# A new hand-written order of all instructions in a fused attention and MLP kernel

## The chip, the cores and the metric

The kernel runs on one core of a Trainium2 chip. The metric is the device time of one execution in microseconds (us); lower is better. A core has five engines that run their own instruction streams in order: TensorE (PE, with its weight loads PEld), VectorE (DVE), ScalarE (ACT), GpSimd (POOL) and SyncE (SP). Here SP only issues DMAs; ACT and POOL issue a few as well. A difference of 0.2%, 1.45 us here, is about what a measurement of this kernel can tell from none.

## What is computed

Block-sparse attention over 4 batches, 8 heads, 768 positions of 64 dimensions, and then an MLP on its output (3072 tokens of 512 features). A block of 32 queries sees its own and the neighbouring blocks, the first and the last block, and three sampled blocks whose numbers are an input; the first and the last block see everything.

```python
scores = scale * np.matmul(q, k.transpose(0, 1, 3, 2))
scores = np.where(mask, scores, -1000000000.0)
attn = np.exp(scores - max);  attn = attn / (sum + 1e-09)
x = (attn @ v).reshape(B * S, H * D)
h = x @ w_in
g = h * np.clip(h + 3.0, 0.0, 6.0) / 6.0
return g @ w_out
```

## The kernel before

All addresses, tiles and operations are fixed in small classes (lines 330 to 727); the order in which they are emitted is one long string, SCORE (line 45), and that string is all that sets the order on every engine and every DMA queue. A phrase names a piece of work and its steps:

```python
for phrase in SCORE.split(";"):
    who, *ops = phrase.split()
    for op in ops:
        works[who[0]][int(who[1:])].do(op)
```

Each engine call is wrapped so that it keeps this order on its engine (Ordered, line 308). An engine thus runs its own steps in the order of the string, and waits where the data or the buffer of the next step is not there yet, with everything behind it on that engine waiting too. How the steps of different engines stand to each other in the string matters only where they share data or a buffer.

The pieces are these.
- **k, Index (line 337).** samp and table load the sampled block numbers; index (line 355) is nine small VectorE instructions that turn them into block numbers for the gathers.
- **c0 to c21, Cache (line 377).** The keys and values of one group of queries, in a ring of two buffers (RING = 2), so cache n waits for the jobs of cache n - 2. kw, vw, kg, vg are plain loads. kc and kf copy keys from the cache before (kc_1 on VectorE). kr and vr gather the three sampled blocks: they first read three block numbers into registers of the issuing engine, from the raw numbers (kr_101, kr_011) or from index's result, and then issue three DMAs. vr reads the registers itself only if kr of the same block has not done so before it (line 431: `regs = self.regs.get(t) or registers(...)`).
- **q, Group (line 437).** A load of the queries and their scaling.
- **j0 to j43, Job (line 459).** Attention of 64 queries: s (32 small matmuls into two PSUM banks), mx (maxima, VectorE), e (exponentials, ACT), then either t and ca or cv (transposes through TensorE and a copy, j0 to j15) or tr and mv (transposes on VectorE and four DMAs, from j16 on), av (64 small matmuls), dn, ml, x, xh, xl (division and the split into a high and a low part). **d0 to d7, Dense (line 561)** do the same for the blocks that see everything, in two halves (s_0, s_1).
- **w0 to w31, Weight (line 660).** A weight arrives as float64 in one of three stage buffers (load, 512 KB), size (ACT) and bits_0, bits_1, bits_2 (VectorE) turn it into float32.
- **m0 to m95, Step (line 682).** 6 units of 512 tokens times 16 slices of the hidden layer: wh and wl split a weight tile into high and low (ACT; GpSimd, in some cases VectorE), h_0 and h_1 are 12 matmuls into the one PSUM bank `hid`, ga, gb, gh, gl make the activation and its two parts (ACT, VectorE, ACT, GpSimd), o_0 to o_3 are three matmuls each into the four OUT banks, which collect 16 steps. oc, os copy a finished bank out (os in two halves on ACT and VectorE), od, oe store it.

Which engine does a step stands in its digits: xl_1 and wl_x1 are VectorE's, xl_0 and wl_x0 GpSimd's; load_1 and k.._1.. are issued by ACT, 0 by SP, vw_2. and kw_2. by POOL. m0 needs the outputs of j0 to j7, so TensorE's dense matmuls can start only when eight jobs are through.

Of the kernel before, what the change touches and what calls it, by code (L numbers as in the profile page):

```python
# [56 lines left out]
    e_00; j4 t_1; j5 e_01; m1 wh_1; j3 av_1; q3 qs_0; j4 ca_0; j3 dn; c3 vw_20 vw_01; j6 s; j3 ml; w4 load_0; j5 e_10;  # L57
    c3 vr_01; c4 kw_20; w0 size; j5 t_0; j6 mx_0; c3 vw_22; j6 mx_1 e_00; c3 vr_00; j6 e_01; m1 wl_10; j3 x; j4 cv_1;
    j6 t_0; j3 xh; j5 ca_0; j4 av_0; j3 xl_1; c4 kr_000; w0 bits_0; j5 e_11; j4 av_1; w2 bits_2; j6 e_10; j5 t_1; j6
    e_11 cv_0; j2 xh; j6 t_1; j4 dn; j2 xl_1; c4 kw_01; j6 ca_1; w0 bits_1; q4 load_0; j5 ca_1; j7 s; w0 bits_2; c4  # L60
    kr_010; w4 size; j4 ml; m0 wh_0; w4 bits_0; j5 av_0; j7 mx_0; j5 av_1; j7 mx_1 e_00; c4 vw_01; j7 e_01; j5 dn; j4
    x; j7 e_10; c4 vw_02; j7 t_0; m1 wh_0; w5 load_0; j5 ml; w4 bits_1; j6 av_0; j4 xh; j7 ca_0; w4 bits_2; j6 av_1;
    j7 e_11; c4 vr_00; j4 xl_1; j7 t_1; j6 dn; j5 x; j6 ml; j5 xh; c4 vw_00; j7 ca_1; j6 x; j5 xl_0; j7 av_0; m0
    wl_01; q4 qs_0; j7 av_1; j6 xh; j7 dn ml; j8 s; c4 vr_01; j7 x; j6 xl_1; j7 xh; j8 mx_0; j7 xl_0; w6 load_0; j8
    mx_1 e_00; m1 wl_00; q5 load_0; m0 h_0; j8 e_01; w8 load_0; c5 kw_01; j8 e_10; c5 kw_20; j8 e_11 t_0; w5 size; j8
    t_1; m0 h_1; j8 ca_0; w5 bits_0 bits_1; j8 ca_1; j9 s; m0 ga gb; j8 av_0 av_1; j9 mx_0; m0 gh; m1 h_0; w5 bits_2;
    m0 gl; w6 size; j8 dn; w7 load_0; j9 mx_1; m1 h_1; c5 kr_010; j9 e_00 e_01; w6 bits_0; m2 wh_0; m0 o_0; m1 ga; m2
    wl_01; m0 o_1; j9 e_10; w6 bits_1; c5 kr_000; w8 size; m0 o_2; m1 gb; q5 qs_0; j9 t_0; w8 bits_0; m0 o_3; j9 e_11;
    w8 bits_1; m1 gh; j9 t_1; w6 bits_2; m2 h_0; m1 gl; j8 ml; m3 wh_0; w9 load_0; j8 x; w7 size; m3 wl_01; m2 h_1; j9
    ca_0; w7 bits_0; j9 ca_1; w8 bits_2; m1 o_0; m2 ga; w7 bits_1; j9 av_0; w10 load_0; m2 wh_1; j9 av_1; m2 gb; j10  # L70
    s; j9 dn; m2 gh; w7 bits_2; m4 wh_0; m1 o_1; m2 gl; j10 mx_0; w11 load_0; w9 size; c6 vw_00; m3 h_0; j10 mx_1; c5
    vw_00; j10 e_00; m4 wl_01; j10 e_01; c5 vw_02; m1 o_2; j10 e_10; c5 vr_00; w9 bits_0; j10 e_11; j9 ml; j10 t_0; w9
    bits_1; w10 size; m1 o_3; w9 bits_2; j10 ca_0; m3 h_1; m2 wl_11; w12 load_0; c5 vw_01; w10 bits_0; j10 t_1; c5
    vr_01; w10 bits_1; m3 ga; m2 o_0; w10 bits_2; m2 o_1; m3 gb; m5 wh_0; c6 kw_00; m2 o_2; j9 x; w11 size; w14
    load_0; m4 h_0; q6 load_0; j10 ca_1; w11 bits_0; c6 kr_000; w11 bits_1; m3 gh; m4 h_1; m3 gl; w12 size bits_0; m2
    o_3; m4 ga; m5 wl_01; j11 s; m3 wh_1; m4 gb wh_1; j10 av_0; m3 wl_11; m4 gh; j10 av_1; w11 bits_2; m5 h_0; j9 xh;
    m4 gl; j10 dn; j8 xh; w13 load_0; j11 mx_0; c6 kr_010; m5 h_1; j11 mx_1 e_00; j9 xl_0; w14 size; m4 wl_10; j11
    e_01; m3 o_0; w14 bits_0; q6 qs_0; c6 kw_01; m3 o_1; j11 e_10; j8 xl_1; m3 o_2; j11 e_11; w14 bits_1; m5 ga; j11
    t_0; w12 bits_1; m3 o_3; j11 ca_0; w12 bits_2; m4 o_0; w14 bits_2; m6 wh_0; w16 load_0; m4 o_1; m5 gb; w13 size;
    w15 load_0; m4 o_2; c6 vw_01; m6 wl_01; m5 wh_1; j11 t_1; m7 wh_0; w13 bits_0; m4 o_3; w13 bits_1; m5 gh; m6 h_0;  # L80
    w13 bits_2; j11 ca_1; m5 gl; j10 ml; w17 load_0; j10 x; j12 s; c6 vr_00; w16 size; m7 wl_01; m5 wl_10; m6 h_1; j12
    mx_0; w16 bits_0; j12 e_00; j11 av_0; w15 size; w16 bits_1; j11 av_1; m6 ga; w16 bits_2; m5 o_0; j12 e_01; m6 gb;
    w18 load_0; m5 o_1; c6 vw_02; j11 dn; m6 gh; c6 vr_01; j11 ml; m5 o_2; w17 size; j11 x; m6 gl; j12 t_0 mx_1; m5
    o_3; w17 bits_0; j12 e_10; q7 load_0; m7 h_0; w15 bits_0; m6 wh_1; w15 bits_1; j12 e_11; w15 bits_2; m8 wh_0; m7
    h_1; m6 wl_11; m7 wh_1; w19 load_0; w17 bits_1; m6 o_0; m7 ga; w17 bits_2; j12 t_1 ca_0; m6 o_1; m7 gb; w20
    load_0; j12 ca_1; c7 kw_00; m7 wl_11; j12 av_0; m7 gh; c7 kr_000; j12 av_1; m8 wl_01; j11 xh; m7 gl; j13 s; j10
    xh; q7 qs_0; m8 h_0; w18 size; j13 mx_0; c7 kw_01; w18 bits_0; j13 e_00; w18 bits_1; m6 o_2; j13 e_01; w19 size;
    j12 dn; m8 h_1; w18 bits_2; w19 bits_0; m9 wh_0; w21 load_0; m6 o_3; j10 xl_1; c7 kr_010; m8 ga; j12 ml; m9 wl_00;
    m7 o_0; j13 mx_1; m7 o_1; m8 gb; j13 e_10 e_11; w19 bits_1; j13 t_0; m8 wh_1; c7 vw_00; m9 h_0; j11 xl_1; c7
    vw_02; m8 gh; w19 bits_2; w20 size; m8 gl; j12 x; j13 t_1; w22 load_0; m9 h_1; j13 ca_0; c7 vr_00; w20 bits_0  # L90
# [731 lines left out]
```

## Time and profile before

| | us |
|---|---|
| median of three runs | 726.73 |
| the runs | 725.34, 726.73, 726.80 |
| the profiled execution | 728.81 |
| its span, first to last instruction | 727.0 |
| TensorE busy in it | 685.3 |
| VectorE, ScalarE, GpSimd busy | 378.7, 372.7, 370.9 |
| moved by DMA | 123.54 MB, mean 170 GB/s |

The span is what the profile shows; the profiled execution's own time has 1.8 us more around it, and it is 2.1 us above the median of the runs. TensorE is the busy engine, but matmuls are pipelined and overlap in the records, so its share says only where it stands still, not how fast it is. The page cuts the span into slices; below, stretches are chosen by hand, and time is counted from the first instruction.

### The profile page before, as it was taken

Reading aid. Unit: us, or ns where it says so; the run is one execution under the profiler, and the core shown is the slowest. Engines: PE = TensorE matmul, PEld = TensorE weight load, DVE = VectorE, ACT = ScalarE, POOL = GpSimd, SP = SyncE. Lnnn points to the kernel's source line nnn. Section 1 sums busy time; section 2 is a strip of 40 time slices with the busy share of each in tenths; the row PEclk is TensorE's granted clock in tenths of the full one; section 3 lists DMA queues with packets and bytes.
Section 4 is the critical chain, followed back from the end, with each engine's and each line's share of the span. In section 5 each row is a group of like instructions: output and inputs, shape, how many; then the busy total and the mean of one; then the engine's idle time right before and its main releaser. Section 6 shows DMA issues by size and latency. Waiting matters only on the chain.

```text
span 727.0 us, 19157 instructions
## 1 busy us (share of the span) xinstructions
PE 685.3 (94%) x7552; PEld 524.3 (72%) x7552; DVE 378.7 (52%) x782; ACT 372.7 (51%) x735; POOL 370.9 (51%) x301
## 2 busy tenths in 40 slices
...
GB/s 258 252 247 254 249 280 263 260 255 215 216 259 122 199 196 162 155 191 207 166 217 124 183 229 139 176 140 154 181 209 219 162 81 60 1 58 1 2 0 59
DMA packets 83118, 123.54 MB, mean 170 GB/s; under 512 B 10707, under 2 KB 61524, under 8 KB 83028
## 3 DMA queue, kind: packets, MB, share of 16 engines
...
q10 hardware_dynamic: 2048, 2.76, 1.1%
...
## 4 chain that ended last, share of the span: by engine, by line
PE 80%; DVE 6%; DMA 5%; SPq 4%; ACT 3%; issue 2%; ACTq 0%; DVEq 0%
PE hid L316 34%; PE out L316 33%; PE bank L316 8%; PE small L316 6%; SPq L316 4%; ACT p L316 1%; DMA stage<-w_out 1%; DVE m L316 1%; DVE w_in L316 1%; DMA pT<-p 1%; DMA stage<-w_in 1%; DMA kp<-kG 1%; DMA vp<-vG 1%; DVE rec L316 1%; DVE g L316 1%
## 5 line engine op out<-in xcount | busy, mean ns | idle before, releaser
L316 PE MATMUL hid<-x,whi 128*128 128x512 f32 x768 | 241.0, 395 | 2.1 <-ACT x L316 0.9
L316 POOL TENSOR_TENSOR glo<-g,ghi 128x512 fp32r<-128x512 f32 x96 | 128.2, 1336 | 150.9 <-ACT ghi L316 147.3
L316 POOL TENSOR_TENSOR wlo<-w_out,whi 128x512 fp32r<-128x512 f32 x90 | 117.7, 1308 | 112.1 <-ACT whi L316 96.4
L316 DVE SCALAR_TENSOR_TENSOR g<-g,hid 128x512 f32<-128x512 f32 x96 | 65.7, 685 | 207.4 <-ACT g L316 207.3
L316 PEld LDWEIGHTS hid<-x,whi 128*128 128x128 f32 x768 | 141.9, 188 | 38.8 <-issue 2.8
L316 PE MATMUL out<-whi,ghi 128*128 128x512 f32 x384 | 155.1, 404 | 0.0
L316 PE MATMUL out<-whi,glo 128*128 128x512 f32 x384 | 149.8, 390 | 0.0
L316 PE MATMUL hid<-x,wlo 128*128 128x512 f32 x384 | 149.7, 390 | 0.0
L316 PE MATMUL out<-wlo,ghi 128*128 128x512 f32 x384 | 149.7, 390 | 0.0
L316 ACT ACTIVATE g<-hid,half_b 128x512 f32<-128x512 f32 x96 | 66.0, 688 | 154.2 <-PE hid L316 130.5
L316 POOL TENSOR_TENSOR wlo<-w_in,whi 128x512 fp32r<-128x512 f32 x88 | 114.6, 1305 | 54.7 <-ACT whi L316 35.8
L316 ACT ACTIVATE p<-bank,m 128x256 f32<-128x256 f32 (+1 forms) x196 | 88.6, 492 | 60.1 <-DVE m L316 51.1
L316 DVE TENSOR_REDUCE m<-bank 128x2 f32<-128x512 f32 (+1 forms) x114 | 70.9, 643 | 47.9 <-PE bank L316 47.6
L316 PEld LDWEIGHTS out<-whi,ghi 128*128 128x128 f32 x384 | 72.0, 188 | 25.3 <-issue 10.1
L316 PEld LDWEIGHTS out<-whi,glo 128*128 128x128 f32 x384 | 72.1, 188 | 15.6
L316 PEld LDWEIGHTS hid<-x,wlo 128*128 128x128 f32 x384 | 72.1, 188 | 15.5
L316 PEld LDWEIGHTS out<-wlo,ghi 128*128 128x128 f32 x384 | 72.2, 188 | 13.2
L316 ACT CAST ghi<-g 128x512 fp32r<-128x512 f32 x96 | 59.6, 621 | 35.2 <-DVE g L316 24.0
L316 ACT CAST whi<-w_out 128x512 fp32r<-128x512 f32 x96 | 59.4, 620 | 30.7 <-PE out L316 26.9
L316 ACT CAST whi<-w_in 128x512 fp32r<-128x512 f32 x96 | 59.4, 619 | 28.1 <-PE hid L316 23.1
L316 DVE STREAM_TRANSPOSE p<-p 128x512 f32<-128x512 f32 (+1 forms) x88 | 54.8, 646 | 24.1 <-ACT p L316 20.9
L316 PEld LDWEIGHTS small<-vp,pT 128*32 128x32 f32 x2816 | 43.6, 110 | 24.8 <-issue 17.5
...
## 6 DMA issues: line engine op xcount, KB each, us to landing
vp<-vG SPq DMA_DIRECT2D x174, 130.0 KB, 3.3
...
kp<-kG SPq DMA_DIRECT2D x39, 256.0 KB, 3.5
stage<-w_in SPq DMA_DIRECT2D x16, 512.0 KB, 4.1
stage<-w_out SPq DMA_DIRECT2D x15, 512.0 KB, 4.4
...
```

Of the source, the lines that this page charges most:

```text
L316: return lambda *a, **k: tc.keep_in_program_order(op(*a, **k))
```

## The change

Only the string SCORE is replaced. The 2822 steps in it are the same 2822 with the same digits, so every operation keeps its engine, its tile and its queue; their order is new throughout. Of the diff the opening, the stretch around d3 to j24, and the end are shown; lines with a minus come first.

```diff
@@ -43,232 +43,201 @@
 SCORE = """
-    q0 load_1; c1 vw_21; k0 samp_0; q1 load_1; k0 table_0; c0 kw_10; k0 ident_0; w3 load_1; c0 kw_11 vw_11 kr_101
-    kr_011; k0 index; q1 qs_0; c1 kw_11; c0 vw_00 vw_02; w3 size; c0 kg_0; q0 qs_0; c1 kr_010 kc_1; w1 load_0; c1
-    vw_00; c0 vr_00; c1 kr_000; j1 s; j0 s; c0 vr_01; j0 mx_0; j1 mx_0; j0 e_00; w1 size; j0 mx_1; c0 vg_0; j0 e_01;
-    w1 bits_0; w2 load_0; c1 kf_0; w3 bits_0; j0 t_0; j1 mx_1; j0 e_10; c2 kw_01; j1 e_00; j0 cv_0; c2 kr_000; j0
-    e_11; w3 bits_1; j1 e_01; j0 t_1; j1 e_10 t_0 e_11; j2 s; j0 ca_1; c2 kr_010; j3 s; j0 av_0; j3 mx_0; c1 vw_02; j1
-    t_1; c2 kc_1; q2 load_0; j2 mx_0; c3 kw_01; j0 av_1; c1 vg_0; j2 e_00; c3 kr_010; w2 size; j2 e_01; w2 bits_0; j3
-    e_00; j2 mx_1; j1 cv_0; j2 e_10; c1 vr_00; j2 e_11; j3 mx_1; j2 t_0; j3 e_01; w1 bits_1; j2 ca_0; j0 dn; c1 vr_01;
-    q2 qs_0; j0 ml; w3 bits_2; j1 av_0; j3 e_10; j0 x; j3 t_0; c3 kr_000; j1 cv_1; j4 s; w1 bits_2; w2 bits_1; m0
-    wh_1; j1 av_1; j4 mx_0; j0 xh; m0 wl_10; j3 e_11; j2 t_1; j3 cv_0; c2 vw_02; w0 load_0; j1 dn; j2 ca_1; q3 load_0;
-    j1 ml; c2 vr_01; j3 t_1; j1 x; c3 kc_1; j1 xh; j2 av_0; j4 mx_1; j3 ca_1; j2 av_1; j4 e_00; j1 xl_1; c2 vw_01; j0
-    xl_1; j5 s; j4 e_01; c2 vr_00; j2 dn; j4 e_10; j2 ml; j4 e_11; j2 x; j4 t_0; j5 mx_0; c2 vw_00; j3 av_0; j5 mx_1
...
-    d3 loadk_1; m30 wh_1; d2 dn; m30 gh gl; m31 h_1; d2 ml; m30 wl_10; m29 o_0; d2 x; m31 ga; d3 s_0 loadv_1; d1 xl_0;
-    c11 kw_00 vg_0; d3 mx_00 mx_10 e_00 e_10 s_1 tr_00 tr_10; m29 o_1; d3 loadv_0 mx_01 mv_0; m29 o_2; d3 mx_11 e_01;
-    m29 o_3; m31 gb; d3 e_11 fd; m30 o_0; m31 gh; d3 tr_01 fe; m30 o_1; m31 gl; d2 xh; d3 tr_11; m33 wh_0; j22 s; d3
-    mv_1; m31 wh_1; m30 o_2; m31 wl_10; j22 mx_0; m30 o_3; j22 mx_1; m32 wl_00; m31 o_0; q13 load_0; j22 e_00; m31 o_1
-    oc_0; j22 e_01; d3 av_00; j22 e_10; m31 od_0; d3 av_10; j22 e_11; c12 vg_0; j23 s; j22 tr_0 tr_1; j23 mx_0; d3
-    av_01; j22 mv; d3 av_11; j23 mx_1 e_00; m31 o_2; j23 e_01; d3 dn; j23 e_10; q13 qs_0; c11 vw_01; j23 e_11; d3 ml
-    x; j24 s; m31 o_3; d2 xl_1; d3 xh; m32 wh_1; d3 xl_1; j24 mx_0; m32 h_0 wl_10; j24 mx_1; j23 tr_0; m32 h_1; m33
-    wl_00; j24 e_00; j23 tr_1; j24 e_01 e_10; j22 av_0; j23 mv; j24 e_11; j22 av_1; m32 ga; j25 s; m33 wh_1; m32 gb;
...
-    gb; m93 o_1; m94 wl_10 gh; m95 h_0; m94 gl; m95 h_1; m93 o_2; m95 ga; m93 o_3; m95 gb; m94 o_0; m95 wh_1 gh; m94
-    o_1; m95 wl_11; m94 o_2; m95 gl; m94 o_3; m95 o_0 o_1 oc_0 o_2 oc_1 od_0 o_3 os_2 oe_2 od_1 os_3 oe_3
+    w3 load_1 size; k0 table_0; w3 bits_0; c0 kw_10 kw_11; w3 bits_1; c1 kc_1; k0 ident_0 samp_0; c1 vw_21; c0 kr_101;
+    q1 load_1; c0 vw_02; k0 index; c0 vw_00; c1 vr_00 vr_01; c0 kg_0 vg_0 kr_011; q0 load_1 qs_0; j1 s; j0 s; j1 mx_0;
+    j0 mx_0; q1 qs_0; j0 e_00 mx_1 e_10; c1 kw_11; j1 mx_1; j0 e_11; j1 e_00; j0 e_01; j1 e_11; j0 t_0; c1 kr_010; w1
+    load_0; c1 vw_00; c0 vr_00; c1 vg_0 kr_000; c2 kw_01; c0 vr_01; j1 e_01; c1 kf_0; c0 vw_11; j0 t_1 cv_0; j1 t_0; j2
+    s mx_0 mx_1; j1 cv_0; j2 e_00; j1 e_10; w1 size; j3 s; w1 bits_0; c2 kc_1; j0 ca_1; j2 e_11; w0 load_0; c1 vw_02; c2
+    kr_000; c3 kr_000; q2 load_0; j3 mx_0; c3 kc_1; w3 bits_2; j1 t_1; j0 av_0 av_1; j1 cv_1; w1 bits_1; j0 dn; w1
+    bits_2; j3 mx_1; c2 kr_010; q3 load_0; j3 e_00; j2 e_10 e_01 t_0 ca_0; j3 e_01 t_0; j2 t_1; w0 size bits_0; j0 ml x
+    xh; j1 av_0 av_1 dn; j3 e_11; j1 ml; q2 qs_0; j2 ca_1; w2 load_0; c3 kr_010; j4 s; c2 vw_00 vr_00; c3 kw_01; j2 av_0
+    av_1; c2 vw_01; j3 cv_0; w2 size; j4 mx_0 mx_1; j0 xl_1; j2 dn; j3 e_10; j5 s; j4 e_00; m0 wh_1; j4 e_01 e_11; j1 x
+    xh; j4 e_10; j3 t_1 ca_1; j4 t_0; w4 load_0; c2 vw_02; w2 bits_0; j2 ml; w2 bits_1 bits_2; j2 x xh; q3 qs_0; j3
+    av_0; j4 t_1; j3 av_1; w0 bits_1 bits_2; j3 dn; j4 ca_0; j1 xl_1; j6 s mx_0 mx_1 e_00 e_10 e_11 e_01; c2 vr_01; j6
+    t_0; c3 vw_01 vr_00; j3 ml; j5 mx_0; c3 vr_01; j3 x; j5 e_00; j3 xh; j2 xl_1; j5 mx_1; q4 load_0; c3 vw_22; j4 cv_1;
+    c4 kr_010; j6 t_1; c4 kw_20; j6 cv_0; j5 e_01 t_0; j4 av_0 av_1; j5 e_10; m0 wh_0 wl_01; j6 ca_1; j4 dn ml; j3 xl_1;
+    c4 kr_000; j7 s; j4 x; j7 mx_0; w4 size; j5 e_11 t_1; m1 wh_1; j5 ca_0; j4 xh; j5 ca_1 av_0 av_1; j7 mx_1; j5 dn; j7
...
+    av_10 mv_1 av_01 av_11 dn; c11 vw_00; d3 loadk_1; c11 vw_01; d2 ml; d3 loadk_0; c12 kr_010; m28 o_2; d2 x; m31 h_0
+    h_1; d3 s_0 mx_00; c12 vw_00; d3 mx_10; m30 gh; m29 wl_10; m30 gl; m29 o_3 o_2; m30 wh_1; m31 ga; m30 wl_10; d3
+    loadv_0; m31 gb; d3 e_00 e_10 tr_00 tr_10; d1 xh; m29 o_0; d1 xl_0; d3 s_1; m30 o_3; d3 mx_01 mx_11 fd e_01 e_11
+    tr_01 tr_11; m29 o_1; c12 kr_000; m30 o_1; q12 qs_1; m31 wh_1; d3 mv_0; m31 wl_10; j22 s; d3 loadv_1 mv_1; m30 o_0
+    o_2; m31 gh gl o_0; j22 mx_0 mx_1; d2 xh; j22 e_00; m31 o_1; j22 e_01 e_11 e_10; d3 fe; j22 tr_0 tr_1; j23 s; q13
+    load_0; j23 mx_0 mx_1; c13 kr_010; d3 av_00 av_01 av_11; m32 wh_0; d3 av_10 dn ml x; j23 e_00 e_01 e_10; d2 xl_1;
+    j23 e_11; q13 qs_0; m31 o_3 o_2; d3 xh xl_1; m32 wh_1 wl_00; j22 mv; m33 wh_0; j24 s mx_0; m32 h_0 h_1; j24 e_00
...
+    wl_10 o_3; m94 ga; m95 wh_0 wl_00; m94 gb; m92 o_2 o_0; m93 o_1 o_2; m95 h_0 h_1; m94 gh wh_1 gl wl_10; m93 o_0; m95
+    ga wh_1 gb; m94 o_3 o_0 o_2 o_1; m79 od_0; m95 wl_11 gh gl o_3 o_0 os_3 oe_3 o_2 os_2 oc_0 od_0 o_1 oc_1 od_1 oe_2
 """
```

In the new opening the load of w3 and its size stand first on ACT, ahead of c0's two key windows (kw_10, kw_11). On VectorE w3's bits_0 and bits_1 and the copy c1 kc_1 stand ahead of index. On SP c1's gathers vr_00 and vr_01 stand ahead of c0's kg, vg and kr_011, and ahead of c1's own kr. From m0 h_0 on, TensorE's stream comes back from a step of attention to h or o 67 times in the new order and 79 times in the old one. Between d3 s_0 and d3 s_1 TensorE has no step before and three o after; between j23 s and j24 s it has d3 av_01, d3 av_11 and one o before, four d3 av and two o after. On VectorE m54 gb stood directly behind d4 dn, d4 ml, j30 xl_1 and d4 x; now it stands directly behind m53 gb, with d4 ml and d4 x after it. At the end, the last output bank is o_1 with oc_1 (one copy, one store of 256 KB) in place of o_3 with os_3 (two half copies, two stores).

## Rows read from the trace of the kernel before

**Rows 1.** Three stretches: length; busy PE, PEld, DVE, ACT, POOL; clock; DMA share; GB/s.

```profile
0.00:67.50 67.50, 37.85 (x864) 23.68 (x864) 36.00 (x89) 29.95 (x66) 6.15 (x12) 0.92 0.79 251
67.50:80.00 12.50, 12.19 (x144) 9.34 (x144) 7.28 (x15) 8.44 (x18) 4.25 (x4) 1.00 0.90 300
80.00:722.00 642.00, 635.04 (x6546) 491.28 (x6544) 334.62 (x678) 333.90 (x652) 360.48 (x285) 1.00 0.54 159
```

**Rows 2.** Waits of PE from 80 us on: us in total, times, longest.

```profile
PE small L316 <- DMA pT<-p: 2.2, 5, 0.7
PE bank L316 <- DMA kp<-kG: 1.5, 1, 1.5
PE bank L316 <- ACT p L316: 1.3, 1, 1.3
PE bank L316 <- DVE rec L316: 0.9, 1, 0.9
PE hid L316 <- DVE g L316: 0.9, 2, 0.6
```

**Rows 3.** The chain that ended last, whole span: start, us, engine, what, matmuls.

```profile
189.18 2.72 PE hid L316 x12
...
210.12 2.95 PE hid L316 x12
```

**Rows 4.** Timelines of DVE, then POOL, at 161 to 182 us: start, us, what.

```profile
163.19 1.79 DVE L316 SCALAR_TENSOR_TENSOR w_in<-stage,w_in 128x512 int32<-128x512 int32 x1
...
179.59 1.41 DVE L316 SCALAR_TENSOR_TENSOR w_out<-stage,w_out 128x512 int32<-128x512 int32 x2
...
163.14 1.30 POOL L316 TENSOR_TENSOR glo<-g,ghi 128x512 fp32r<-128x512 f32 x1
...
169.43 1.74 POOL L316 TENSOR_TENSOR glo<-g,ghi 128x512 fp32r<-128x512 f32 x1
```

**Rows 5.** Timeline of the start, all engines; in brackets idle time before and what ended it.

```profile
3.18 0.47 DVE L316 TENSOR_TENSOR p<-p 1x72 f32<-1x72 f32 x2 [0.99 <-DMA p<-table]
...
4.62 0.18 DVE L316 CAST blocks<-p 1x72 int32<-1x72 f32 x1
...
11.15 2.76 SPq L316 DMA_DIRECT2D kp<-kG  x4
11.51 0.43 DVE L316 COPY kp<-kp 128x512 f32<-128x512 f32 x1 [6.71 <-DMA kp<-kG]
...
13.71 0.64 ACT L316 ACTIVATE w_out<-stage 128x512 f32<-128x512 f32 x1
```

**Rows 6.** The page's DMA issues: queue, count, KB each, median us to landing.

```profile
vp<-vG SPq DMA_DIRECT2D x174, 130.0 KB, 3.3
...
kp<-kG SPq DMA_DIRECT2D x39, 256.0 KB, 3.5
...
stage<-w_out SPq DMA_DIRECT2D x15, 512.0 KB, 4.4
...
stage<-w_out ACTq DMA_DIRECT2D x1, 512.0 KB, 8.0
```

**Rows 7.** Timeline of SP's queue, 20 to 75 us: issues of one kind merged.

```profile
32.99 1.39 SPq L316 DMA_DIRECT2D kp<-kG  x3
34.56 4.58 SPq L316 DMA_DIRECT2D vp<-vG  x6
...
51.77 3.80 SPq L316 DMA_DIRECT2D vp<-vG  x6
...
64.90 4.47 SPq L316 DMA_DIRECT2D vp<-vG  x7
```

**Rows 8.** Timeline of PE, 47 to 84 us: j8's av.

```profile
72.96 1.27 PE L316 MATMUL small<-vp,pT 128*32 128x65 f32 x64
```

**Rows 9.** The chain that ended last, 712 to 727 us.

```profile
720.24 0.70 DVE stage L316
...
722.97 0.41 DVE p L316
```

More of the change, by code (lines that the diff above doesn't have):

```diff
@@ L56 @@
-    xl_1; j5 s; j4 e_01; c2 vr_00; j2 dn; j4 e_10; j2 ml; j4 e_11; j2 x; j4 t_0; j5 mx_0; c2 vw_00; j3 av_0; j5 mx_1
[L57 to L90, printed above, removed]
```

343 lines of the change are left out of this document (172 added, 171 removed).

## The prediction

> **What bounds the kernel now.** I read the stretches first. In the first 67.5 us TensorE is busy for 37.9, so 29.7 us are lost before its first dense matmul (m0 h_0). From 67.5 to 80 us it loses 0.3, and in the 642 us up to the end of its work 7.0 [rows 1]. So there are three stocks of time: the head, the waits in the long dense part, and what TensorE spends inside its busy time. A tail of some 5 us after the last matmul, of which the last copy starts at 722.97 [rows 9], is the fourth. VectorE is busy for half of the long stretch and bounds nothing by its share.
>
> Next the waits of TensorE. Of the 7.0 us, 2.2 are waits for transposed probabilities that come back by DMA, 1.5 is one wait for keys, 1.3 is d3 s_1 waiting for ACT to empty the banks of s_0, 0.9 is j24 s, and 0.9 is h_0 of two steps waiting for VectorE's gb [rows 2]. That is nearly all that a better order of the dense part can win from waits.
>
> Inside the busy time the chain shows a price of order itself. Twelve matmuls of h take 2.72 us with dense neighbours and 2.95 us where a step of attention stands before or behind [rows 3]. One excursion from dense work to attention and back costs 0.23 us.
>
> Last, what the title speaks of. A VectorE operation with two inputs in SBUF, bits of a weight, takes 0.7 us free (two in 1.41), but one took 1.79 us while GpSimd ran a glo beside it from 163.14 to 164.44 [rows 4]. VectorE waits for GpSimd there. Such stretched operations lie ahead of two of TensorE's waits, the one for keys (SP waits for a stage buffer that VectorE frees) and m55 h_0; but these are at most 1.5 + 0.9 us [rows 2]. However much VectorE waits in all, TensorE feels only that.
>
> **The change, part by part.** Operations and engines are the same, so only position has a price.
>
> *Switches.* From m0 on TensorE comes back to dense work 67 times and not 79. 12 x 0.23 = 2.8 us; seven of the twelve are excursions to a transpose only, which may cost less than an excursion to the small matmuls of s and av. Between all twelve at full price (2.8) and five alone (1.2) I take **-2.5**, nearer the row.
>
> *Waits of TensorE.* Three o (3 x 0.68 = 2.0 us, as 0.68 is a quarter of the 2.72 of twelve matmuls) now stand between d3 s_0 and s_1, where none stood and 1.3 us was waited: gone. Two more d3 av and one more o, over 1.3 us, stand between j23 and j24, where 0.9 was waited: gone. m54 gb no longer stands behind d4's and j30's steps on VectorE: 0.6 of the 0.9 gone. The wait for keys is gone if VectorE's weight work runs without stretches: 1.5. The 2.2 us for probabilities hang on SP's queue, which is just as full there: they stay. Sum 4.3; the ends are 0 (new waits as large as the old) and 7.0 [rows 1]. I take **-4.3**, the rows that have a reason.
>
> *The head.* This part speaks against the change. SP's queue paces the head: it issues gathers almost without a pause, at about 0.65 us each (3.80 for six) [rows 7]. The value gathers of c4 are its last burden: the last of seven is issued near 64.90 + 4.47 - 0.5 = 68.9 and lands 3.3 us later [rows 6, 7], at 72.2, and j8's av starts at 72.96 [rows 8]. The slack is 0.8 us; whatever SP is late beyond that TensorE is late.
> Before, index ended at 4.8 us, and SP issued c0's kg and c1's gathers from 11.15 on, behind c0's other loads [rows 5]. In the new order index stands on VectorE behind w3's bits and c1 kc_1, and kc_1 needs c0 kw_11, which ACT issues only behind w3 size. The steps: w3's load issued at about 1, 4.4 us to land [rows 6]; size 0.64 [rows 5]; two key loads issued, the second landing some 4 us later (0.5 + 3.5 [rows 6]); kc_1 0.43; index about 1.8 (1.6 from 3.18 to 4.80 and the first instruction) [rows 5]. Sum 12.3. Until then SP has only two value loads to issue, and vr_00 waits. So SP begins its long run 1.1 us later than before. On it now lie c0's kr_011, which before went out in SP's first 5 us, and two register reads that c1's vr needs because kr comes after it. A kg, a register read and a kr take 2.76 together [rows 5]; three kr take 1.39 [rows 7]; less another 0.46 for kg the register read is 0.9. Added: 0.9 + 1.39 + 2 x 0.9 = 4.1. SP is late by 1.1 + 4.1 = 5.2 us, TensorE by 4.4.
> What can give it back: six gathers took 4.58 us at 34.56 and 3.80 at 51.77 [rows 7], so some issues are held up by transfers still under way, and the head moves 251 GB/s where the next stretch reached 300 [rows 1]. A queue that starts later may run with fewer such holds. Lower end 0. Upper end: the only load of a weight on ACT's queue took 8.0 us and not 4.4 [rows 6], which makes it 4.4 + 3.6 = 8.0. I take **+2.5**, a little over half of 4.4, because the late bursts ran free of holds already. The first scores then start near 23 us instead of 15; that alone costs nothing, as SP, not TensorE, sets the pace there.
>
> *The tail.* The last copy is a whole one (0.70) in place of a half (0.41) [rows 9], and the last store is 256 KB in place of 128: +0.3 and an estimated 0.2, **+0.5**; between 0.3 and 1.
>
> Sum: -2.5 - 4.3 + 2.5 + 0.5 = -3.8 us on the profiled execution, 728.8 to 725.0. It lies 2.1 us above the median of the runs, so **722.9 us** against 726.73.
>
> **A rule weighed against the trace.** GpSimd is stretched too: a glo took 1.74 us beside VectorE's weight bits and 1.30 otherwise [rows 4]. The Trainium skill, SBUF — State Buffer, "Who interferes with whom", says the shared port pair is an exclusive lock, held by whichever of the two started first while the other fully blocks. The 1.79 and the 1.74 agree with it in both directions. By that rule an order that spares VectorE by starting it first hands the wait to GpSimd, whose gl and wl feed o and h; the sum would then be B's below, not the forecast's.
>
> **Rivals.**
> *A, slower: SP's late start is not given back.* Place: SP's queue between index and c4's vr. With w3 landing as slowly as its one example the head costs 8.0, and weights, which come through the same queue, are late too, so that the wait for keys stays (waits -2.8): 8.0 - 2.5 - 2.8 + 0.5 = +3.2, 729.9 us. It decides the sign from a head of 2.5 + 4.3 - 0.5 = 6.3 us on. For it: index stands behind three foreign steps, with two landings in the path. Against: the holds on SP's queue. Chance 0.21.
> *B, no change: the waits only move,* from VectorE to GpSimd or to other places of a string that is new throughout; the switches pay for the head: 2.5 - 2.5 + 0.5 = +0.5, 727.2 us. For it: GpSimd's 1.74 [rows 4], the new order has three steps whose first o comes five o behind h_1 (5 x 0.68 = 3.4 us), and the tightest before has six (4.1), and the change may not spare VectorE any wait at all. Chance 0.18.
> *C, faster: the head is covered.* The holds give the whole 4.4 back: -6.3, 720.4 us; with the 2.2 for probabilities gone as well, 718.2. For it: 251 against 300 GB/s. Chance 0.21.
> The forecast keeps 0.40.
>
> **How the numbers follow.** The time is the forecast's, 722.9. The range runs from C with its extra, 718, to a little past A, 731. What a measurement can tell is 0.2%, 1.45 us: the forecast and C lie below that, B within, A above: 0.61 faster, 0.18 same, 0.21 slower.
>
> **What would show it.** Right: a first matmul near 23 us, m0 h_0 between 68 and 72, j8 av waiting for values; PE's idle time after 80 us near 3 us; fewer stretched DVE operations; no wait of d3 s_1 or j24 s. Wrong: m0 h_0 at 75 or later (A), or a list of new PE waits behind glo or wlo that adds up to 7 us (B). If VectorE's stretches vanish and TensorE's waits do not shrink, the title's aim was not where the time was.

## The result, and the profile after

The new order takes 736.88 us (median of four executions, 732.71 to 738.95), the old one beside it 726.64 (725.34 to 726.80): ratio 1.0129, interval 1.010 to 1.0157. It is slower by some 10 us, where 722.9 was predicted and 731 was the end of the range.

The two profiled executions show less than half of that: 728.81 before, which is 2.2 above this median, and 732.71 after, the fastest of its four. The two profiles are read first; what other profiles make of them stands behind.

Three stretches of the new order, cut at its own m0 h_0, with the columns of [rows 1]:

```profile
0.00:73.30 73.30, 37.73 (x865) 22.87 (x865) 36.19 (x88) 29.42 (x65) 6.65 (x13) 0.98 0.76 237
73.30:80.00 6.70, 6.28 (x116) 4.34 (x116) 3.38 (x6) 5.40 (x11) 1.69 (x3) 1.00 0.82 256
80.00:726.50 646.50, 641.79 (x6582) 495.98 (x6573) 332.82 (x690) 337.81 (x660) 358.61 (x287) 1.00 0.54 160
```

TensorE's busy time in the head is the same (37.73 against 37.85), but the head is 5.8 us longer. In the long stretch TensorE stands still for 4.71 us, of which 0.75 lie behind its last matmul (it ends at 725.75); that leaves 3.96 instead of 6.96. The waits of PE from 80 us on, which answer to [rows 2]:

```profile
PE hid L285 <- ACT x L285: 1.2, 1, 1.2
PE hid L285 <- DVE g L285: 0.9, 3, 0.4
PE small L285 <- DMA vp<-vG: 0.8, 1, 0.8
PE small L285 <- issue: 0.6, 2, 0.3
PE small L285 <- DMA pT<-p: 0.5, 2, 0.3
PE bank L285 <- ACT q L285: 0.4, 1, 0.4
```

The waits of d3 s_1, of j24 s and for keys are gone. But m32 h_0, directly behind j24 s, now waits 1.2 us for ACT's x, and this list leaves something out. The timeline of the start and of d6 (start, us, engine, what; answers to [rows 5, 7, 8]):

```profile
0.74 0.40 ACTq L285 DMA_DIRECT2D stage<-w_out  x1
1.89 13.99 SPq L285 DMA_DIRECT2D vp<-vG  x8
4.43 0.66 ACT L285 ACTIVATE w_out<-stage 128x512 f32<-128x512 f32 x1 [1.98 <-DMA stage<-w_out]
8.05 0.43 DVE L285 COPY kp<-kp 128x512 f32<-128x512 f32 x1 [1.77 <-DMA kp<-kG]
10.04 0.18 DVE L285 CAST blocks<-p 1x72 int32<-1x72 f32 x1
17.99 3.67 SPq L285 DMA_DIRECT2D kp<-kG  x6
19.27 1.11 PE L285 MATMUL out<-kp,q 64*32 64x256 f32 x16 [19.27 <-DMA kp<-kG]
...
68.89 5.16 SPq L285 DMA_DIRECT2D vp<-vG  x7
...
73.26 0.77 PE L285 MATMUL hid<-x,whi 128*128 128x512 f32 x2
...
470.76 5.44 SPq L285 DMA_DIRECT2D pT<-p  x8
475.99 1.72 PE L285 MATMUL small<-stage,pT 128*32 128x65 f32 x30
477.99 1.21 PE L285 MATMUL small<-stage,pT 128*32 128x65 f32 x66 [0.28 <-DMA pT<-p]
...
479.93 0.62 PE L285 MATMUL hid<-x,whi 128*128 128x512 f32 x2
```

Index ends at 10.22 us (before: 4.80), and SP, which has only two value loads to issue before it, issues c1's six gathers only then; c0's keys come behind them, from 15.92 to 19.4. The last gathers of c4 are issued from 68.89 on (64.90 before) and m0 h_0 starts at 73.26 (67.51 before). At d6 the row of 30 small matmuls takes 1.72 us, the 66 behind it 1.21: the 30 hold a wait that the list of waits does not count, because it lies inside a row of matmuls.

Where the time stands in each profile, read from TensorE's timeline (start of the hid matmuls of m0 and m32, start of the last out matmuls); the names are those of the experiments below:

| kernel | m0 h_0 at | m0 h_0 to m32 h_0 | m32 h_0 to the last o |
|---|---|---|---|
| old order | 67.5 | 238.5 | 415.4 |
| new order | 73.3 | 235.3 | 416.3 |
| new again (e3) | 72.8 | 235.7 | 419.2 |
| new, index first (e4) | 70.3 | 235.8 | 420.8 |
| new, SP's order mended (e6) | 67.5 | 235.0 | 418.5 |
| old head, new rest (e1, e14) | 65.9, 65.7 | 237.1, 236.5 | 420.0, 417.8 |
| new head, old rest (e2) | 74.7 | 237.9 | 413.6 |
| new from m1 to m32 alone (e7, e15) | 66.3, 66.3 | 236.5, 237.4 | 413.7, 414.2 |

So on the profiled pair: head +5.75, dense part -2.3 (238.5 + 415.4 against 235.3 + 416.3), from the last o to the end +0.4 (5.6 and 6.0): +3.9, the difference of the spans (727.0, 730.9). Over all profiles, however, the new order behind m32 takes 416.3 to 420.8 us, mean 418.8 of six, and the old one 413.6 to 415.4, mean 414.2 of four. The pair caught the fastest of the one and the slowest of the other.

The heads of the pair mislead in the same direction: in the table m0 h_0 stands at 66.3 us in the mean of the five with the old head, where the profile before has 67.5, and at 73.6 in the mean of the three with the unchanged new one (after, e3, e2). By such means the new order loses 7.3 us in the head, wins 2.0 from there to m32 (236.2 in the mean of eight against 238.2 of two), and loses 4.6 behind m32 and 0.4 in the tail. That is +10.3, and the medians lie 10.2 apart.

### The profile page after: what moved, and what is told of

Its sections match the earlier page's. It is cut to its first block, busy times and chain, and to the rows that moved or that the text cites. A ratio compares the mean times of both kernels' runs of the same rounds, so it can differ in the third digit from the quotient of the medians.

```text
span 730.9 us, 19177 instructions
## 1 busy us (share of the span) xinstructions
PE 685.8 (94%) x7552; PEld 523.2 (72%) x7552; DVE 373.0 (51%) x782; ACT 372.6 (51%) x735; POOL 366.9 (50%) x301
## 4 chain that ended last, share of the span: by engine, by line
PE 84%; DMA 5%; SPq 4%; DVE 3%; ACT 2%; issue 2%; POOL 0%; DVEq 0%; ACTq 0%
PE hid L285 35%; PE out L285 34%; PE bank L285 8%; PE small L285 7%; SPq L285 3%; DMA kp<-kG 2%; DMA stage<-w_in 1%; DVE m L285 1%; ACT p L285 1%; SPq L339 1%; DMA pT<-p 1%; DMA vp<-vG 1%; DMA stage<-w_out 1%; DVE p L285 0%; DMA q<-qT 0%
## 5 line engine op out<-in xcount | busy, mean ns | idle before, releaser
L285 POOL TENSOR_TENSOR glo<-g,ghi 128x512 fp32r<-128x512 f32 x96 | 125.3, 1305 | 144.4 <-ACT ghi L285 134.8
L285 ACT ACTIVATE g<-hid,half_b 128x512 f32<-128x512 f32 x96 | 65.9, 687 | 108.3 <-PE hid L285 92.2
L285 ACT ACTIVATE p<-bank,m 128x256 f32<-128x256 f32 (+1 forms) x196 | 86.6, 490 | 67.6 <-DVE m L285 58.0
```

The lines of the kernel that those rows point to most:

```text
L285: return lambda *a, **k: tc.keep_in_program_order(op(*a, **k))
```

## The experiments

**Which part costs what.** The old string up to m0 h_0 and the new one behind it (e1), the reverse (e2), and the new string once more (e3). Steps that one string has already done are left out of the other.

```diff
-    w3 load_1 size; k0 table_0; w3 bits_0; c0 kw_10 kw_11; w3 bits_1; c1 kc_1; k0 ident_0 samp_0; c1 vw_21; c0 kr_101;
...
+    q0 load_1; c1 vw_21; k0 samp_0; q1 load_1; k0 table_0; c0 kw_10; k0 ident_0; w3 load_1; c0 kw_11 vw_11 kr_101
...
```

> The old order up to m0 h_0, the new order for everything behind it. Theory 1 (SP's late queue in the new head costs 5.8 us, and the new dense part is 2 us shorter): m0 h_0 at 67.5 us as in the old order, first matmul at 15, dense part 651.6 long, the profiled execution near 727; against the kernel before -1.5 us, ratio 0.998, and its runs as close together as those of before. Theory 2 (the new dense part is slower in most executions, the profiled one excepted): m0 h_0 at 67.5 too, but the median stays 3 us or more above before, ratio 1.004 or more, with runs 4 to 6 us apart. If the weights' place in the head matters for the first unit, waits of PE appear between 80 and 185 us.

Measured: 729.89 us (12 executions), ratio 1.0032, interval 1.0009 to 1.0054, executions from 726.7 to 732.5.

The reverse, against the old order, at the seam:

```diff
-    mx_1 e_00; m1 wl_00; q5 load_0; m0 h_0; j8 e_01; w8 load_0; c5 kw_01; j8 e_10; c5 kw_20; j8 e_11 t_0; w5 size; j8
+    s; j7 xl_0; j8 mx_0 mx_1; m0 h_0; m1 wh_0; w4 bits_2; c4 vr_01; w6 load_0; j8 e_00; m1 wl_00; q5 load_0; j8
...
```

> The new order up to m0 h_0, the old order for everything behind it. Theory 1 (the head is the whole loss, and its lateness also makes what hangs on SP's queue vary from run to run): m0 h_0 near 73.3, first matmul near 19.3, dense part 653.9 as in the old order, time of before + 5.8 in the profile, ratio 1.008 to 1.014. Theory 2 (the head costs 5.8, the rest of the 10 us lies in the new dense part): ratio 1.008, with runs 1.5 us apart.

Measured: 733.89, ratio 1.0101 (1.0067 to 1.0134), executions from 733.3 to 736.7.

The new order, with no edit:

> The new order unchanged, for another profile and more times. The first profile (732.7) was 4 us below the median of the runs (736.9). Theory 1 (head): a profile of a slower execution has m0 h_0 later than 73.3 by the difference, with the dense part at 651.6. Theory 2 (dense part): m0 h_0 near 73.3 and a dense part of 654 to 658, in which the list of PE waits after 80 us is longer than 4.7 us. Theory 3 (clock): m0 h_0 and the waits as before, with half-clock stretches that the first profile did not have.

Measured: 736.27, ratio 1.0137 (1.0101 to 1.0174).

The head costs 6.4 us (736.27 - 729.89) or 7.4 (733.89 - 726.51), the rest 3.4 (729.89 - 726.51) or 2.4 (736.27 - 733.89). Both theories hold a part: the head is the larger loss, and the new dense part loses too, in most executions though not in the first profile. The second profile of the same program shows where. d6 again, with the windows (columns as above) around it:

```profile
470.28 5.41 SPq L292 DMA_DIRECT2D pT<-p  x8
475.48 1.12 PE L292 MATMUL small<-stage,pT 128*32 128x65 f32 x28
476.85 0.30 PE L292 MATMUL small<-stage,pT 128*32 128x65 f32 x2 [0.25 <-DMA pT<-p]
478.99 2.16 PE L292 MATMUL small<-stage,pT 128*32 128x65 f32 x66 [1.84 <-DMA pT<-p]
...
482.40 0.62 PE L292 MATMUL hid<-x,whi 128*128 128x512 f32 x2
```

```profile
475.00:480.00 5.00, 2.91 (x73) 1.98 (x75) 1.02 (x2) 1.83 (x3) 3.96 (x4) 0.88 0.66 174
480.00:485.00 5.00, 5.00 (x53) 4.05 (x45) 0.00 (x0) 0.00 (x0) 0.80 (x1) 0.78 0.47 147
```

SP issues the eight transfers of d6's probabilities one behind the other, until 475.69. TensorE arrives at 475.48, before the last is issued, and goes on at 478.99; in the first profile the last was issued by 476.20 and TensorE went on at 477.99. What the transfer takes to land, 1.8 us or 3.3, falls on TensorE in full. In the old order SP is through at 469.5 and TensorE arrives at 472.11, and the same 96 matmuls are one row:

```profile
464.12 5.39 SPq L316 DMA_DIRECT2D pT<-p  x8
...
472.11 1.57 PE L316 MATMUL small<-stage,pT 128*32 128x65 f32 x96
```

From the first start of these 96 to the last it is 1.35 us in each of the four profiles with the old rest, and 3.0 to 5.4, in the mean 4.1, in the six with the new one: 2.7 of the 4.6 us behind m32 are lost at this place.

The mix that keeps the new order only where it was shorter:

```diff
-    t_1; m0 h_1; j8 ca_0; w5 bits_0 bits_1; j8 ca_1; j9 s; m0 ga gb; j8 av_0 av_1; j9 mx_0; m0 gh; m1 h_0; w5 bits_2;
+    gb; j8 av_0 av_1; j9 mx_0; m0 gh; m1 h_0; j9 mx_1; m0 gl o_3; j9 e_00 e_01 e_11; j8 dn ml; j9 e_10; m2 wh_0
...
-    x; j24 s; m31 o_3; d2 xl_1; d3 xh; m32 wh_1; d3 xl_1; j24 mx_0; m32 h_0 wl_10; j24 mx_1; j23 tr_0; m32 h_1; m33
+    wl_00; j22 mv; m33 wh_0; j24 s mx_0; m32 h_0; m31 oc_0 od_0; m32 wl_10; j24 mx_1; j23 tr_0; m32 h_1; m33 wl_00;
...
```

> The old order up to m1 h_0, the new order up to m32 h_0, the old order from there. By the waits and returns of each unit in the profiles, the new order is 1.7 us shorter in the first two units and 3 to 5 us longer in the four others. If these sums hold for executions in general, the time is 1.5 to 2.5 below before, 724.5, ratio 0.997. Rival (the seams bring new waits, or the first units' gain is chance): 726 or more.

Measured: 723.53, ratio 0.9959 (0.9944 to 0.9974): faster than both orders. It was run a second time, beside a second run of e1's kernel, with no edit in either:

> The old head and the new rest again, as in the first such run: ratio 1.003 (1.001 to 1.0055), dense part near 657 with 2.8 to 3.5 us waited at d6.

> The mix of the old order and the new one's first two units again: ratio 0.996 (0.9945 to 0.9975). Against the old head with the new rest in the same job 4.5 to 6.5 us less; by the profiles' sums over the units behind m32 (waits and returns 3.3 + 4.8 against 10.5 + 4.3, and 0.4 of tail) it should be 6.8.

Measured: 730.81, ratio 1.0065 (1.0042 to 1.0088), which is past the 1.0055 expected, and 724.68, ratio 0.9978 (0.9963 to 0.9993). From m1 to m32 both run the new order, so the 6.1 us between them (6.4 between the first two) lie behind m32 and in the tail; in the table it is 3.6 and 6.3 behind m32, and 0.4 in the tail.

**The head.** One move on VectorE (e4), then two more on SP (e6).

```diff
-    w3 load_1 size; k0 table_0; w3 bits_0; c0 kw_10 kw_11; w3 bits_1; c1 kc_1; k0 ident_0 samp_0; c1 vw_21; c0 kr_101;
-    q1 load_1; c0 vw_02; k0 index; c0 vw_00; c1 vr_00 vr_01; c0 kg_0 vg_0 kr_011; q0 load_1 qs_0; j1 s; j0 s; j1 mx_0;
+    w3 load_1 size; k0 samp_0 table_0 index; w3 bits_0; c0 kw_10 kw_11; w3 bits_1; c1 kc_1; k0 ident_0; c1 vw_21; c0
+    kr_101; q1 load_1; c0 vw_02 vw_00; c1 vr_00 vr_01; c0 kg_0 vg_0 kr_011; q0 load_1 qs_0; j1 s; j0 s; j1 mx_0; j0
```

> The new order with one move: samp, table and index stand ahead of w3 bits_0, bits_1 and c1 kc_1 on VectorE. If index's place is what makes SP late, vr_00 goes out about 5 us earlier than 11.4, the first scores come before 19.3, m0 h_0 falls to 68 to 69.5, and the time is 4 to 5 us below the new order's. Rival: SP's extra burden (kr_011 and c1's register reads on its long run, 4 us) is what counts: m0 h_0 stays at 72 or more, time at most 1.5 us below the new order's.

Measured: 732.29, ratio 1.0074 (1.0049 to 1.01), 4.0 us below the new order of the same job.

```diff
-    kr_101; q1 load_1; c0 vw_02 vw_00; c1 vr_00 vr_01; c0 kg_0 vg_0 kr_011; q0 load_1 qs_0; j1 s; j0 s; j1 mx_0; j0
+    kr_101; q1 load_1; c0 vw_02 kr_011 vw_00 kg_0 vg_0; q0 load_1 qs_0; j1 s; j0 s; j1 mx_0; j0 mx_0; q1 qs_0; j0
...
+    c0 vr_00; c1 vg_0 kr_000; c2 kw_01; c0 vr_01; c1 vr_00 vr_01; j1 e_01; c1 kf_0; c0 vw_11; j0 t_1 cv_0; j1 t_0;
```

> The new order with the three things on SP's path in the head undone and nothing else: index ahead of w3's bits; c0 kr_011 ahead of c0's other loads, where SP is idle; c1 vr_00 and vr_01 behind c1's kr and c0's vr, so that they need no register reads of their own. Index alone left m0 h_0 at 70.3, 4.4 above the old head on the same chip (65.9). If the rest is SP's extra burden of 4.1 us, m0 h_0 falls to 66 to 67.5 and the time to 730, 6 us below the new order. Rival (the other engines' new places in the head matter): m0 h_0 stays at 69 or more, time 732 or more.

Measured: 731.10, ratio 1.0083 (1.0055 to 1.011). SP's queue and m0 h_0 in the timelines, first of e4, then of e6:

```profile
1.83 10.31 SPq L292 DMA_DIRECT2D vp<-vG  x8
14.29 3.69 SPq L292 DMA_DIRECT2D kp<-kG  x6
...
70.32 1.22 PE L292 MATMUL hid<-x,whi 128*128 128x512 f32 x2
```

```profile
3.80 1.53 SPq L292 DMA_DIRECT2D kp<-kG  x3
...
9.56 2.64 SPq L292 DMA_DIRECT2D kp<-kG  x3
...
67.53 1.22 PE L292 MATMUL hid<-x,whi 128*128 128x512 f32 x2
```

With index first, c1's gathers end 3.7 us earlier (12.14 against 15.88) and m0 h_0 comes 2.5 to 2.9 us earlier. With the two moves on SP it stands where the old order has it, though every other engine keeps its new order of the head. In the times the second step cannot be told from none (1.0074 and 1.0083, intervals that overlap); its 2.8 us are shown by one profile each. By the ratios e6 still lies 1.3 to 3.7 us above the old head with the new rest (1.0065 and 1.0032). So the times show index's place as a cause, worth 4.0 us; SP's two moves are shown in the profiles alone, and that the other engines' places cost nothing is not shown.

**The dense part behind m32.** Three changes at d6, all on the kernel of e1. First TensorE's side:

```diff
-    o_0; m55 o_1; m59 wh_0; m57 wh_1 ga gb; j31 xl_1; d6 av_00 av_01 av_10; m59 wl_00; m58 wl_00; m57 gh; d6 av_11;
-    d7 loadk_0; m56 o_3; m58 h_0 h_1; c16 vw_02; d7 loadk_1 s_0 mx_00 e_00 mx_10 e_10 tr_10; m57 gl wl_10; d7 tr_00;
+    o_0; m55 o_1; m59 wh_0; m57 wh_1 ga gb; j31 xl_1; m59 wl_00; m58 wl_00; m57 gh; d7 loadk_0; m56 o_3; m58 h_0
+    h_1; d6 av_00 av_10 av_01 av_11; c16 vw_02; d7 loadk_1 s_0 mx_00 e_00 mx_10 e_10 tr_10; m57 gl wl_10; d7 tr_00;
```

> The old head and the new rest once more (730 us, 3.4 above before), with one move on TensorE: the four d6 av stand behind m56 o_3, m58 h_0 and m58 h_1, 3.4 us later, and both that need mv_0 stand first. Three of four profiles of the new rest wait 2.8 to 3.5 us there, for the last transfers that SP issues at about the moment at which TensorE arrives. Theory 1 (that place is the main loss of the new dense part): the wait is gone and does not come back at d7, time 2.5 to 3.5 below the old head with the new rest, so 727, ratio 1.000. Rival (the wait only moves, to m58 h_0 behind m57 gb or to d7's scores and outputs): under 1 us gained.

Measured: 730.66, ratio 1.0066 (1.0048 to 1.0085): nothing won. The timeline has the two places named for the rival:

```profile
470.83 0.73 PE L294 MATMUL hid<-x,whi 128*128 128x512 f32 x2 [1.40 <-DVE g L294]
...
473.78 1.57 PE L294 MATMUL small<-stage,pT 128*32 128x65 f32 x96
475.28 0.86 PE L294 MATMUL bank<-stage,q 64*64 64x384 f32 x4
478.38 0.86 PE L294 MATMUL bank<-stage,q 64*64 64x384 f32 x4 [2.24 <-DMA stage<-kD]
```

The av are one clean row now, but m58 h_0 waits for gb, and d7 s_0 for keys: their load needs the stage buffer that d6's av read (SP issues it at 475.38, when the av are through). Then SP's side, in two steps:

```diff
-    o_1; c16 vr_00; c17 kr_000; c16 vw_01 kr_000; d6 loadv_1; c16 kw_00; d6 tr_00 mx_01 fd e_01 e_11 tr_01 tr_11; d5
-    dn; d6 mv_0; m55 o_2; m57 h_0; d6 mv_1; m56 wh_1; m58 wh_0; d6 fe; m56 gh wl_10 gl; m55 o_0 o_3; m57 h_1; m56
+    o_1; c16 vr_00; c17 kr_000; d6 loadv_1 tr_00 mx_01 fd e_01 e_11 tr_01 tr_11; d5 dn; d6 mv_0; m55 o_2; m57 h_0;
+    d6 mv_1; c16 vw_01 kr_000 kw_00; m56 wh_1; m58 wh_0; d6 fe; m56 gh wl_10 gl; m55 o_0 o_3; m57 h_1; m56 o_0; m55
```

> The old head and the new rest (730 us), with SP's queue relieved at d6 in place of TensorE: c16 vw_01, kr_000 and kw_00 (five issues, some 2.5 us) stand behind d6 mv_1, and d6 av_10 ahead of av_01. Moving the av themselves brought nothing, because d7's keys then waited for the buffers. Theory (SP issues d6's probabilities too late): mv_0 goes out at the end of tr_00, about 1.2 us earlier, mv_1 1.2 to 1.5 earlier, and the wait at d6 falls from 3.5 to 1 to 2 us; time 1.5 to 2 below the old head with the new rest, 728.3, ratio 1.002. Rival (landing time varies by more than that, or c16's gathers then hold up a later job): under 0.7 us.

Measured: 728.15, ratio 1.0021 (1.0001 to 1.0041). The av no longer wait, but d7's scores do, for 1.64 and 0.91 us in the profile, since c16's five issues now stand ahead of d7's keys. The next step puts them into the gap in which SP waits for d6's av:

```diff
-    d6 mv_1; c16 vw_01 kr_000 kw_00; m56 wh_1; m58 wh_0; d6 fe; m56 gh wl_10 gl; m55 o_0 o_3; m57 h_1; m56 o_0; m55
+    ga gb; j31 xl_1; d6 av_00 av_10 av_01; m59 wl_00; m58 wl_00; m57 gh; d6 av_11; d7 loadk_0; c16 vw_01 kr_000; m56
+    o_3; m58 h_0 h_1; d7 loadk_1; c16 kw_00 vw_02; d7 s_0 mx_00 e_00 mx_10 e_10 tr_10; m57 gl wl_10; d7 tr_00; m56
```

> The old head and the new rest, with SP's queue alone changed at d6 and d7: c16 vw_01 and kr_000 between d7 loadk_0 and loadk_1, where SP waits for d6's av, c16 kw_00 and vw_02 behind loadk_1; d6 av_10 ahead of av_01. If c16's place on SP's queue is the cause there, neither d6 av (3.5 us) nor d7 s (3.5 us in the two earlier tries) waits for more than 1 us, and the time is 2 to 3 below the old head with the new rest in the same job. If the passage is too short on TensorE whatever SP does, 2 us or more of waits stay at d7 s and less than 1 us is won.

Measured: 728.13, ratio 1.0022 (1.0006 to 1.0038), 2.7 us below e14 of the same job.

```profile
460.84 5.15 SPq L294 DMA_DIRECT2D pT<-p  x8
...
467.54 1.57 PE L294 MATMUL small<-stage,pT 128*32 128x65 f32 x96
...
472.70 1.63 PE L294 MATMUL bank<-stage,q 64*64 64x384 f32 x8
```

SP is through with d6 at 466.0, 1.5 us before TensorE arrives, and d6's av are one clean row; d7's scores take 1.63 us where 0.88 is usual, which leaves a wait of 0.75 there. From m32 to the last o it takes 416.4 us where e1 and e14 took 420.0 and 417.8. In the times this is level with e9 (1.0022 and 1.0021): what the two share, d6's transfers ahead of c16's gathers, is what was won, and the second step is worth nothing that can be measured. So the place of c16's gathers on SP's queue, ahead of d6's transfers, costs about half of the 4.6 us behind m32: 2.7 us in the times, 1.4 to 3.6 in the profiles. The other half lies in small waits, none over 1.1 us (j34 to j37 for probabilities, h_0 of m70 and m81 for gb), and was not taken apart.

**The prices of the prediction.** Its waits, on the old order:

```diff
-    m54 ga; m52 o_3; d4 x; d5 av_00; m54 wh_1; d5 av_10; m54 gb wl_10;
+    m54 ga gb; m52 o_3; d4 x; d5 av_00; m54 wh_1; d5 av_10; m54 wl_10;
...
-    d3 e_10 s_1 tr_00 tr_10; m29 o_1; d3 loadv_0 mx_01 mv_0; m29 o_2;
+    d3 e_10; m29 o_1 o_2; d3 s_1 tr_00 tr_10 loadv_0 mx_01 mv_0;
...
-    j24 s; m31 o_3;
+    m31 o_3; j24 s;
```

> The old order with three moves, each at a wait of TensorE that the prediction expected to go: m29 o_1 and o_2 between d3 s_0 and s_1 (1.3 us waited there), m31 o_3 ahead of j24 s (0.9), m54 gb directly behind m54 ga (0.6). Theory 1 of the prediction (a wait is won by putting ready matmuls in front of it): 2.8 us won, 723.7, ratio 0.996. Rival (these places lie on chains through other engines, and the wait moves to the next step of the chain, d3 av or m32 h_0): under 1 us, with new waits of the same size at d3 av and m32 h_0.

Measured: 725.16, ratio 0.9987 (0.9975 to 1.0): 0.9 us by the ratio, 1.5 by the medians, of the 2.8. The waits of PE from 80 us on:

```profile
PE bank L321 <- DMA kp<-kG: 1.3, 1, 1.3
PE small L321 <- DMA pT<-p: 1.2, 3, 0.5
PE hid L321 <- ACT x L321: 0.9, 1, 0.9
PE hid L321 <- DVE g L321: 0.2, 1, 0.2
PE bank L321 <- DVE rec L321: 0.2, 1, 0.2
```

d3 s_1's wait is gone and m55 h_0's too. j24 s waits 0.2 instead of 0.9, and m32 h_0 behind it 0.9 for ACT's x, which was none before: the same chain (d3 av, dn, x, xh) now ends at h_0. That is the wait of 1.2 which the new order has there.

The mix of e7 with the m54 gb move alone:

```diff
-    m54 ga; m52 o_3; d4 x; d5 av_00; m54 wh_1; d5 av_10; m54 gb wl_10;
+    m54 ga gb; m52 o_3; d4 x; d5 av_00; m54 wh_1; d5 av_10; m54 wl_10;
```

> The mix of the old order with the new one's first two units (723.5, 3.1 below before), with one move: m54 gb directly behind m54 ga, where m55 h_0 waits 0.7 us. Expected 0.5 to 0.7 below the mix, 722.9, ratio 0.995; rival: the 0.7 comes back at the next wait (d5's or d6's), ratio 0.996 as without the move.

Measured: 724.22, ratio 0.9972 (0.9951 to 0.9992). Its profile no longer has the wait of m55 h_0, but the time lies between the mix's two results: undecided at this size.

The returns to dense work, 15 edits like this one:

```diff
-    m17 wh_1; j17 av_0; j19 mx_0; j17 av_1; j16 x; m16 o_0; j19 e_00; j17
+    m17 wh_1; j17 av_0; j19 mx_0; j16 x; m16 o_0; j17 av_1; j19 e_00; j17
```

> The old order with 15 more returns to dense work: in 15 jobs the o that stood behind av_1 stands between av_0 and av_1. Same operations, same engines. If a return costs what the prediction took (0.23 us), 15 x 0.23 = 3.5 us are lost: 730, ratio 1.0047. By the floors read from both traces a return costs 0.13 us behind the small operation, and the start of the small one about 0.09 more. Rival (the returns are free, their cost being the wait of whatever comes behind): under 0.7 us.

Measured: 730.86, ratio 1.0053 (1.0034 to 1.0072): 0.26 us per return (0.0053 x 726.3 / 15; 0.16 to 0.35). The rival falls. This is the price of a return from small matmuls whose row is split; returns of other kinds were not tried.

Last, what VectorE's waits for GpSimd are worth, with more than half of GpSimd's work left out:

```diff
         def wl(self, side, engine):
+            if self.n > 1:
+                self.lo[side] = steps[self.n % 2].lo[side]
+                return
```

> The old order without the low parts of the weights from m2 on: the 188 wl (176 on GpSimd, the rest on VectorE, a few less for the first two steps) are left out, and the matmuls read the low parts of m0 and m1, as many and as long as before. GpSimd loses more than half of its work, and VectorE the waits for it. It bounds from above what an order that has VectorE's waits for GpSimd in view could win. If those waits set TensorE's time, 4 us or more are gained (722 or less), and the waits of TensorE for VectorE's g and rec and for keys go. If they do not, as the traces suggest (VectorE's stretches fell from 24 to 19 us in the new order and TensorE gained nothing by it), the time moves by less than 1.5 us.

Measured: 724.70, ratio 0.9979 (0.996 to 0.9999), 1.5 us. Busy times on the page, and the waits of PE from 80 us on:

```profile
PE 684.0 (95%) x7552; PEld 523.9 (72%) x7552; DVE 360.2 (50%) x769; ACT 371.6 (51%) x735; POOL 146.3 (20%) x126
```

```profile
PE bank L316 <- ACT p L316: 1.3, 1, 1.3
PE bank L316 <- DVE rec L316: 0.9, 1, 0.9
PE small L316 <- DMA pT<-p: 0.8, 2, 0.4
PE bank L316 <- PE small L316: 0.2, 1, 0.2
```

GpSimd is left with 20% and TensorE still waits for ACT's p and VectorE's rec as before; those for g and for keys are gone, those for probabilities smaller. One kind of VectorE operation that GpSimd stretches, the 36 xl and their like, shows how little the new order itself changed; the line group of after, then of e10 (before: 634 ns in the mean, 22.7 us):

```profile
L285 DVE TENSOR_TENSOR x<-xt,x 128x256 fp32r<-128x256 f32 (+1 forms) x36 | 19.5, 548 | 6.4 <-ACT x L285 6.3
```

```profile
L316 DVE TENSOR_TENSOR x<-xt,x 128x256 fp32r<-128x256 f32 (+1 forms) x36 | 19.1, 535 | 3.2 <-ACT x L316 3.1
```

In this group the new order took away nearly all that can be taken (548 ns, with 535 when GpSimd is almost idle). Over all VectorE instructions, each against the lower quartile of its own kind and counted from 0.05 us on, the stretches sum to 24.1 us before, 18.9 after and 12.3 in e10. So half of them are still there in e10, and its 1.5 us bound only the half that went, 11.8 us. The new order took away 5.2, less than e10 did: it spared VectorE something, and by this bound that was worth little.

The Trainium skill, SBUF — State Buffer, "Who interferes with whom", holds that issue order decides who blocks. By that rule an order which spares VectorE could hand the wait to GpSimd. The trace of after does not show that: a glo takes 1.29 us in the median in both orders, at most 1.77 before and 1.76 after.

## Why the prediction was wrong, point by point

**The head is the step that failed.** Its mechanism was right and named: index behind foreign steps, c0's kr_011 on SP's long run, two register reads more. SP was put 5.2 us late; the last gathers of c4 go out 4.0 us later at their start and some 4.7 at their end, and in the profiles of e4 and e6 those three moves undo the delay of m0 h_0. Of the two terms of the 5.2 the start (1.1) came out smaller, as c1's first gather went out at 11.36 and not behind 12.3; the added work on SP (4.1) came out whole. What failed is "I take +2.5, a little over half of 4.4", with its reason that a queue that starts later runs with fewer holds. Nothing was given back: m0 h_0 is 5.75 us late in the profile, at 73.3 and past the 68 to 72 that the prediction named, and the head costs 6.4 to 7.4 in the times. The lower end of 0 and rival C rested on that reason and fall with it. The slack of 0.8 us was read at the wrong place as well: j8's av stand behind m0 h_0, which starts before the last gathers of c4 have landed. Ahead of m0 h_0 the old order's TensorE last waits for a gather at j4's av, and in e6 it waits for c4's keys at j8 s (the first row is of before, the second of e6); neither place has slack.

```profile
53.85 1.35 PE L316 MATMUL small<-vp,pT 128*32 128x65 f32 x64 [1.47 <-DMA vp<-vG]
```

```profile
65.51 2.09 PE L292 MATMUL bank<-kp,q 64*32 64x256 f32 x32 [1.83 <-DMA kp<-kG]
```

**The waits, -4.3, failed too.** Each wait named was examined at its own place, and there most of it went: d3 s_1, j24 s, m55 h_0, keys. But what took their place was not priced. j24's 0.9 became m32 h_0's 1.2 (e8 repeats that on the old order), d6 lost 1.6 to 4.0 us on SP's queue, 2.7 in the mean, and the small ones behind m32 fill the rest. By the table the new order is 4.6 us slower behind m32 and 2.0 faster ahead of it: +2.6 where returns and waits together were to bring -6.8. With the returns at about -1 (below) the waits come to some +3.6 in place of -4.3. This is rival B, that waits only move, with the place it left open now named for about half of the loss: SP's queue at d6 and d7.

**The switches, -2.5, were taken too large.** The price holds, 0.26 us per return against 0.23 taken, but e12 paid it for returns from small matmuls, and seven of the twelve that the new order saves are returns from transposes, as the prediction noted. In the traces these cost nothing: an excursion of four transposes takes 0.585 us from the last dense start to the next, one of eight 1.028, so that two short ones (1.17) are as long as a long one and one more dense interval of 0.227, to within the 0.09 by which the first dense interval behind a return is longer. Five returns at 0.26 are 1.3, near the prediction's own lower end of 1.2. An estimate from all seventeen traces, with the lower quartile of each kind of interval between two starts on TensorE, gives 0.9 for the whole order, and 0.2 of it ahead of m32. So the returns are not why the first two units gain and the mix of e7 beats both orders; the waits are: those for keys (1.5) and of d3 s_1 (1.3) are gone there, and j24's 0.9 came back as 1.2. **The tail, +0.5,** measured 0.4.

**The sum on the profiled pair** becomes +5.75 - 2.3 + 0.4 = +3.9. That the medians lie 10 apart is the second error: the forecast was made as if an execution were the kernel. The old order's profile was the longest of four behind m32 (415.4, against 413.6 to 414.2 in the other three) and the latest of five at m0 h_0, and the new order's first profile the shortest of six behind m32, with the shortest wait at d6. The fastest and slowest executions of e14 are 8.5 us apart (726.5 to 735.0), of e13, with d6 mended, 5.7 (724.8 to 730.5); what the slowest did was not profiled and stays open.

**The rivals** A and B were taken as alternatives, each with a chance of its own; both happened, A without its slow load of w3 (issued at 0.74, size starts at 4.43, 3.7 us against the 8.0 feared). A with the whole of B's lost waits would have read 8.0 - 2.5 + 0.5 = +6.0, 732.7, beyond the range.

**The title's aim:** the sign of its wrongness was given ("if VectorE's stretches vanish and TensorE's waits do not shrink"), and e10 bears it out: with more than half of GpSimd's work and half of the stretches gone, 1.5 us.
